# A recurrent attention kernel: the left rows' output projection in matmuls of 512 columns, with six of its passes moved into the next step

## The chip, the cores and the metric

The kernel runs on one core of a Trainium2 chip. The metric is the device time of one execution in microseconds; for the kernel before it is 2106.89 us, the median of three runs (2102.43 to 2125.25). The profile is of one execution with a span of 2098.7 us. TensorE is the engine for matmuls, VectorE, ScalarE and GpSimd work elementwise, and SyncE issues the stream of weights.

## The reference: what is computed

Two independent branches are added to the input. Branch A is an attention layer that walks over 2048 rows in 64 segments of 32 rows. Eight memory rows stand before each segment, and the first eight rows of a segment's output are the next segment's memory. So the segments can only be done one after the other, and each needs all four weight matrices (8 MB each in bf16).

```python
for s in range(n_seg):                                # 64 segments
    xs = x[:, s * seg_len:(s + 1) * seg_len, :]       # 32 rows of 1024
    h = jnp.concatenate([mem, xs], axis=1)            # 8 + 32 rows
    q, k, v = (jnp.einsum('btd,dhe->bhte', h, W) for W in (Wq, Wk, Wv))   # 32 heads of 128
    scores = jnp.einsum('bhqe,bhke->bhqk', q, k) * scale   # then mask and softmax -> p
    o = jnp.einsum('bhqk,bhke->bhqe', p, v)
    o = jnp.einsum('bhte,hed->btd', o, Wo)            # output projection, 4096 -> 1024
    mem = o[:, :M, :]                                 # the next segment's memory
    outs.append(o[:, M:, :])
```

Branch B sends the two rows with the highest router score through a gated feed-forward block, and runs at the kernel's end.

## The kernel before

A step s works on 32 rows that TensorE takes as one block: 8 memory rows and 24 of the segment's rows. The last eight rows of each segment, the **left rows**, are not on the recurrence's path for q, k and v, so they are gathered from four segments (a group G; j = s mod 4) into another block of 32 rows. The left rows' q is computed in the step with j = 2, their k in j = 3, both for the group ahead, and their v in j = 0. Their output projection, `project_left`, is done in the step with j = 3, when the attention of all four segments is there (OTL), into the PSUM tile WL.

The weights are cut into 64 granules of 512 KB (48 for q, k and v in six phases of eight, 16 for Wo). 42 stay in SBUF, 22 are streamed anew in every step, through six slots (tile g). Three of the streamed ones bring only half: the other half is held in PSUM and copied by ScalarE. A slot is loaded again when `used` is called after the last matmul that reads it.

```python
N_RES = 42
N_SLOT = 6
PHASES = [(0, 0), (1, 0), (0, 1), (1, 1), (2, 0), (2, 1)]     # (matrix, half): q, k, q, k, v, v

# one step: the six phases, each of eight granules
for p, (mat, half) in enumerate(PHASES):
    ...
    for kc in range(KC):
        g = 8 * p + kc
        Gv = granule(g)
        for jq in range(4):      # four column groups of the array, 512 columns each
            nc.tensor.matmul(PSm[32 * jq:32 * jq + 32, :], lhsT=ST[:, kc, :], rhs=Gv[:, 512 * jq:512 * (jq + 1)], ...)
        ...                      # a left pass with the same granule, where this step has one
        for fn in hooks.pop((p, kc), []):
            fn()                 # other work, hung in at a place (phase, granule)
    if mat < 2:
        XB = two.tile([P, 512], BF16, tag="xb", name="XB")
        nc.scalar.copy(out=XB[:, :], in_=PSm[:, :])
        hooks.setdefault((p + 1, (3, 2, 3, 2)[p]), []).insert(0, lambda ...: transposes(m, h, b))
```

The output projection comes after the phases. Its matmuls have 256 columns, because four column groups share the 1024 outputs:

```python
def project(PS, w, Gv, lhs, last=False, first=False):
    for hs in range(2):                   # two heads in a granule
        h = 2 * w + hs
        for g in range(4):                # four column groups
            nc.tensor.matmul(PS[32 * g:32 * g + 32, 0:256], lhsT=lhs(h),
                             rhs=Gv[:, D * hs + 256 * g:D * hs + 256 * (g + 1)], ...)

def project_left(w, Gv, WL=WL if j == 3 else None):
    nonlocal n_wl
    project(WL, w, Gv, lhs_left, first=(n_wl == 0))
    n_wl += 1

for w in range(16):
    if w == 4:
        attend(1, 0)                      # value products of the second half of the heads
    if w == 8:
        attend(1, 1)
    Gv = granule(48 + w)
    project(WO, w, Gv, lhs_main, w == 15)
    if j == 3:
        ...
        if 48 + w in streamed:            # w = 0, 2, 5, 8, 11, 14
            project_left(w, Gv)
        else:
            behind.append((w, Gv))        # ten resident ones
        if w in (10, 12, 14):
            project_left(*behind.pop(0))
    used(48 + w)

OB = one.tile([P, 512], BF16, tag="vm", name="OB")
nc.scalar.copy(out=OB[:, 0:P], in_=WO[:, 0:P])
nc.vector.tensor_copy(out=OB[:, P:256], in_=WO[:, P:256])
```

When a step's projection is done, OB must be copied and the memory rows transposed into the next step's operand (`mem_to_st`) before the next step begins. Passes that don't depend on it (`fill`) are put on either side of the transposes: in the steps with j = 3 the seven left passes that remain, with j = 1 and 2 passes of the next step's left q or k.

```python
if j == 3:
    fill = [lambda w=w, Gv=Gv: project_left(w, Gv) for w, Gv in behind]
elif j == 1 or j == 2:
    ...                                   # left q or k passes of the next step
for fn in fill[:len(fill) // 2]:
    fn()
if s + 1 < NSEG:
    mem_to_st(OB, nxt["st"])
for fn in fill[len(fill) // 2:]:
    fn()
if j == 3:
    ...
    def left_store(G=G, WL=WL, X=XLT):
        residual(WL, X[:, 0:256], P, False)          # adds x + xn by four matmuls of 256 columns
        OL = one.tile([P, 512], BF16, tag="vm", name="OL")
        nc.scalar.copy(out=OL[:, 0:256], in_=WL[:, 0:256])
        ...                                          # four stores
    todo += [((0, 6), left_norm), ((1, 6), left_store)]   # places in the next step
```

Of the kernel before, what the change touches and what calls it, by code (L numbers as in the profile page):

```python
# [8 lines left out]
BF16 = mybir.dt.bfloat16  # L9
F32 = mybir.dt.float32  # L10
U32 = mybir.dt.uint32
ALU = mybir.AluOpType
# [15 lines left out]
def kernel(  # L28
# [16 lines left out]
    nc = tc.nc  # L45
    P = 128
    Bsz, S, D = A_x.shape
    H, E = A_Wq.shape[1], A_Wq.shape[2]
    M = A_mem0.shape[1]
    SEG = int(A_seg_len)  # L50
# [8 lines left out]
    XM = SEG - M  # L59
# [32 lines left out]
    two = ctx.enter_context(tc.tile_pool(name="two", bufs=2, reuse_waits="tile"))  # L92
# [8 lines left out]
    IDENT = const.tile([P, P], BF16, name="IDENT")  # L101
# [3 lines left out]
    for q0 in range(0, P, 32):  # L105
        nc.vector.tensor_copy(out=SPREAD[q0:q0 + 32, :, :],
                              in_=IDENT[q0:q0 + 32, q0:q0 + 32].unsqueeze(2).to_broadcast([32, 32, 4]))
# [140 lines left out]
    def load_left(G, queue=nc.gpsimd, again=False):  # L248
        X = two.tile([P, 512], BF16, tag="xb", name="XL") if again else one.tile([P, 512], BF16, tag="vm", name="XL")
        for sl in range(4):  # L250
            r0 = (4 * G + sl) * SEG + XM
            queue.dma_start(out=X[32 * sl:32 * sl + 32, 0:256],
                                in_=x2[r0:r0 + XL, :].rearrange("r (g c) -> (r g) c", g=4))
        return X
# [19 lines left out]
    def norm_left(G, X):  # L274
        PS = psT.tile([P, 2], F32, tag="t", name="PS")
        for b in range(0, P, 32):
            nc.tensor.matmul(PS[b:b + 32, :], lhsT=SPREAD[b:b + 32, 4 * XM:P], rhs=MS[b:b + 32, G, :],
                             start=True, stop=True, tile_position=(b, b), skip_group_check=True)
        norm(X[:, 0:256], X[:, 256:512], PS, P)
# [19 lines left out]
    def residual(PS, Z, n, start):  # L299

        for g in range(4):
            nc.tensor.matmul(PS[32 * g:32 * g + 32, 0:256], lhsT=IDENT[0:n, g::4], rhs=Z, start=start, stop=not start,
                             tile_position=(0, 32 * g), skip_group_check=True)
# [26 lines left out]
    def granule(g):  # L330
        return take("w", g) if g in streamed else res_tiles[g]

    def used(g):
        if g in streamed:
            fetch()
# [9 lines left out]
    todo = []  # L345
# [55 lines left out]
    def left_pass(L, kc, Gv):  # L401

        for jq in range(4):
            nc.tensor.matmul(L["ps"][32 * jq:32 * jq + 32, :], lhsT=cur["stl"][:, kc, :],  # L404
                             rhs=Gv[:, 512 * jq:512 * (jq + 1)], start=(not L["had"]), stop=(len(L["had"]) == KC - 1),
                             tile_position=(0, 32 * jq))
        L["had"].append(kc)

    def left_bank():
        return {"ps": psL.tile([P, 512], F32, tag="accl", name="PSl"), "had": []}  # L410

    begun = {}
    for s in range(NSEG):
        G, j = divmod(s, 4)
# [114 lines left out]
        def attend(half, ph):  # L529
            if half not in OT:  # L530
                OT[half] = one.tile([P, 4, 4, SEG], BF16, tag=("qt", "kt")[half], name="OT")
            PTm, PTl = PTs[half]

            if ph == 0:
                OA[half] = psA.tile([P, 512], F32, tag="acc", name="OA")
            OB1 = psT.tile([P, 4 * NK], F32, tag="t", name="OP")
            c1 = 256 if half == 0 else 256 * ph
            OP = (OA[half][:, c1:c1 + 4 * NK], OB1[:, :])
            for il in range(4):
                for jl in range(2):  # L540
                    q0 = 32 * (2 * ph + jl)
                    c0 = half * 512 + il * P
                    o = OP[jl][:, il * NK:(il + 1) * NK]
                    nc.tensor.matmul(o, lhsT=VM[half][q0:q0 + 32, il * P:(il + 1) * P], rhs=PTm[q0:q0 + 32, il, 0:NK],  # L544
                                     start=True, stop=False, tile_position=(q0, 0), skip_group_check=True)
                    nc.tensor.matmul(o, lhsT=VL[q0:q0 + 32, c0:c0 + P], rhs=PTl[q0:q0 + 32, il, 0:NK],  # L546
                                     start=False, stop=True, tile_position=(q0, 0), skip_group_check=True)
            h0 = 16 * half + 8 * ph
            for jl in range(2):
                ov = OP[jl].rearrange("p (i q) -> p i q", i=4)  # L550
                copy = nc.vector.tensor_copy if half == 1 and jl == 1 else nc.scalar.copy
                copy(out=OT[half][:, 2 * ph + jl, :, :], in_=ov[:, :, 0:SEG])  # L552
                copy(out=OTL[:, h0 + 4 * jl:h0 + 4 * jl + 4, j, :], in_=ov[:, :, SEG:NK])
# [41 lines left out]
        for p, (mat, half) in enumerate(PHASES):  # L595
# [3 lines left out]
            lag, behind = 2 if j == 0 else 0, []  # L599
# [3 lines that stand above are left out]
                for jq in range(4):  # L603
                    nc.tensor.matmul(PSm[32 * jq:32 * jq + 32, :], lhsT=ST[:, kc, :], rhs=Gv[:, 512 * jq:512 * (jq + 1)],  # L604
                                     start=(kc == 0), stop=(kc == KC - 1), tile_position=(0, 32 * jq))
# [40 lines left out]
        if j == 3:  # L646
            WL = psL.tile([P, 512], F32, tag="accl", name="WL")

        def project(PS, w, Gv, lhs, last=False, first=False):
            for hs in range(2):  # L650
                h = 2 * w + hs
                for g in range(4):
                    nc.tensor.matmul(PS[32 * g:32 * g + 32, 0:256], lhsT=lhs(h),  # L653
                                     rhs=Gv[:, D * hs + 256 * g:D * hs + 256 * (g + 1)], start=(first and hs == 0),
                                     stop=(last and hs == 1), tile_position=(0, 32 * g), skip_group_check=True)
# [7 lines left out]

        n_wl, behind = 0, []

        def project_left(w, Gv, WL=WL if j == 3 else None):
            nonlocal n_wl
            project(WL, w, Gv, lhs_left, first=(n_wl == 0))
            n_wl += 1

        for w in range(16):
            if w == 4:
                attend(1, 0)
# [5 lines that stand above are left out]
                if w == 2:  # L679
                    XLT = load_left(G, again=True)  # L680
                if 48 + w in streamed:
                    project_left(w, Gv)
                else:
                    behind.append((w, Gv))
                if w in (10, 12, 14):
                    project_left(*behind.pop(0))
            used(48 + w)

        OB = one.tile([P, 512], BF16, tag="vm", name="OB")
# [8 lines left out]
        todo = [((0, 2), store)]  # L698

        fill = []  # L700
        nl = left_of(s + 1) if s + 1 < NSEG else {}
        if j == 3:
            fill = [lambda w=w, Gv=Gv: project_left(w, Gv) for w, Gv in behind]
        elif j == 1 or j == 2:
            for mat in nl:
                begun[mat] = left_bank()
                fill = [lambda kc=kc, g=8 * mat + kc, L=begun[mat]: left_pass(L, kc, res_tiles[g])
                        for kc in range(KC) if 8 * mat + kc not in streamed]
# [6 lines left out]
        if j == 3:  # L715

            def left_norm(G=G, X=XLT):
                norm_left(G, X)

            def left_store(G=G, WL=WL, X=XLT):  # L720
                residual(WL, X[:, 0:256], P, False)
                OL = one.tile([P, 512], BF16, tag="vm", name="OL")
                nc.scalar.copy(out=OL[:, 0:256], in_=WL[:, 0:256])
                o4 = out2[4 * G * SEG:4 * (G + 1) * SEG, :].rearrange("(s r) d -> s r d", s=4)
                for g in range(4):
                    nc.gpsimd.dma_start(out=o4[:, XM:SEG, 256 * g:256 * (g + 1)], in_=OL[32 * g:32 * (g + 1), 0:256])

            todo += [((0, 6), left_norm), ((1, 6), left_store)]
        if s + 1 < NSEG:
# [12 lines left out]
    for w in range(2):  # L742
# [3 lines left out]
        for kc in range(KC):  # L746
            for fh in range(2):
                Gt = take("gu", w, kc, fh)

                for q in range(4):  # L750
                    nb = 4 if q < 2 else 3
                    nc.tensor.matmul(GU[w, fh][32 * q:32 * q + 32, 0:nb * P], lhsT=XSP[:, kc, :],
                                     rhs=Gt.rearrange("p (b q c) -> p q b c", q=4, c=P)[:, q, 0:nb, :],
                                     start=(kc == 0), stop=(kc == KC - 1), tile_position=(0, 32 * q))
# [10 lines left out]
    for fh in range(2):  # L765
        for p1, c0, c1 in ((P, 0, 3 * P), (64, 3 * P, 4 * P)):
            nc.scalar.activation(out=SG[0:p1, fh, c0:c1], in_=GU[0, fh][0:p1, c0:c1], func=ACTF.Silu)
            nc.vector.tensor_tensor(out=HB[0:p1, fh, c0:c1], in0=SG[0:p1, fh, c0:c1], in1=GU[1, fh][0:p1, c0:c1],
                                    op=ALU.mult)
# [7 lines left out]
    for i in range(FC // 2):  # L777
        Gt = take("dn", i)
        for a in range(2):
            fh, r = divmod(2 * i + a, FC // 2)  # L780
            b, q = divmod(r, 4)
            for dh in range(2):
                nc.tensor.matmul(YP[dh][0:2, :], lhsT=HT[:, 4 * fh + b, q, :],
                                 rhs=Gt[:, a * D + dh * 512:a * D + (dh + 1) * 512],
                                 start=(i + a == 0), stop=(2 * i + a == FC - 1))
        fetch()
    NEW = fin.tile([2, D], BF16, name="NEW")
    for dh in range(2):
        c = slice(512 * dh, 512 * (dh + 1))
# [40 lines left out]
```

## Time and profile before

| what | value |
|---|---|
| time, median of three | 2106.89 us |
| span of the profiled execution | 2098.7 us |
| TensorE busy: matmuls, weight loads | 1740.0 us, 898.2 us |
| VectorE, ScalarE, GpSimd busy | 747.4, 712.7, 540.9 us |
| DMA over the span | 768.74 MB, mean 366 GB/s |
| chain that ended last: DMA, TensorE | 50%, 39% |
| left projection: 2048 matmuls of 256 columns, busy | 58.4 us (resident granules), 44.0 us (streamed) |
| left q, k and v: 3072 matmuls of 512 columns, busy | 183.1 us, 103.1 us |

In the profile, busy times are shares of one engine's own time, and several engines work at once. PE is TensorE's matmuls, PEld its weight loads, DVE is VectorE, ACT ScalarE, POOL GpSimd, SP SyncE, DVEq and the like an engine's sequencer. Matmuls overlap in the array, so a group's busy time is the union of its matmuls, not their sum. "L653" is a line of the kernel; all matmuls of `project` have this one line, and are told apart by the tile that they write (OA for the main rows, which WO is a name of, and WL for the left ones). A wait's releaser is the thing that came last; "issue" is a wait for nothing that the profile shows. The granted clock is the part of full speed that the array had. A step ends, for this text, where the first copy into OB starts; the 64 of them lie from 114.92 to 2037.51 us, 30.5 us apart on average. The tail after the last is the end of branch B.

### The profile page before, as it was taken

The numbers are of one execution on the slowest core, as the hardware profiler recorded it, in microseconds if no ns is written. First come the engines' busy times: TensorE is split into PE (matmuls) and PEld (weight loads), VectorE is DVE, ScalarE is ACT, GpSimd is POOL, SyncE is SP. The second block draws the span as 40 slices with busy tenths as digits, with TensorE's granted clock in tenths as the row PEclk, the third lists the DMA queues.
The fourth block names the chain that finished last, engine by engine and source line by source line (L and its number), as shares of the span: only waits on it lengthen the run. The fifth ranks groups of instructions, "written<-read, shape, count | busy, mean of one in ns | idle before, by whom it ended". The sixth has DMA issues, their size and how long they took to land.

```text
span 2098.7 us, 82755 instructions
## 1 busy us (share of the span) xinstructions
PE 1740.0 (83%) x36202; PEld 898.2 (43%) x36202; DVE 747.4 (36%) x2328; ACT 712.7 (34%) x1738; POOL 540.9 (26%) x1030
## 2 busy tenths in 40 slices
PE   3578898888889888888888888898898889888775
PEld 1234444444444444444444444444454444444341
DVE  5523332333333233333333333332333333333430
ACT  3633333333333333333333333333333333333320
POOL 4422223222222322222132222223222222222210
PEclk8689999999999999999999999999999999999986
DMA  9999999999999999999999999999999999999998
GB/s 356 334 380 384 360 383 352 389 343 377 373 363 382 350 383 345 364 382 356 367 354 391 360 379 373 373 385 344 385 369 363 373 380 391 321 388 356 362 340 343
DMA packets 294351, 768.74 MB, mean 366 GB/s; under 512 B 37458, under 2 KB 42770, under 8 KB 293988
## 3 DMA queue, kind: packets, MB, share of 16 engines
q1 hardware_dynamic: 267652, 732.79, 93.5%
q0 software_dynamic: 23520, 26.06, 3.7%
q8 instruction: 283, 4.64, 0.8%
q10 hardware_dynamic: 2816, 4.59, 0.6%
q14 instruction: 80, 0.66, 0.1%
HBM read 750.68 MB, written 12.59 MB: 364 GB/s over the span
## 4 chain that ended last, share of the span: by engine, by line
DMA 50%; PE 39%; DVE 4%; issue 4%; ACT 2%; POOL 1%; ACTq 0%; DVEq 0%; SPq 0%; POOLq 0%
DMA g<-in_A_Wo_dram 19%; PE PSm L604 18%; DMA g<-in_A_Wv_dram 12%; DMA g<-in_A_Wq_dram 11%; PE PSl L404 6%; PE OA L653 5%; PE WL L653 3%; PE PTq L444 2%; DMA g<-in_A_Wk_dram 2%; DMA XL<-in_A_x_dram 1%; DMA out_dram<-OB 1%; DMA wres<-in_A_Wo_dram 1%; DMA g<-in_B_w_up_dram 1%; PE SPS L488 1%; PE OA L544 1%
## 5 line engine op out<-in xcount | busy, mean ns | idle before, releaser
L604 PE MATMUL PSm<-wres,ST 128*32 128x512 bf16 x8192 | 746.7, 394 | 6.8 <-DVE ST L309 5.1
L604 PE MATMUL PSm<-g,ST 128*32 128x512 bf16 x4096 | 417.1, 394 | 92.1 <-DMA g<-in_A_Wv_dram 42.9
L604 PEld LDWEIGHTS <-ST 128*32 128x32 bf16 x12288 | 294.8, 97 | 422.6 <-issue 192.3
L653 PEld LDWEIGHTS <-OT 128*32 128x32 bf16 x8192 | 221.6, 99 | 167.1 <-issue 151.7
L220 ACT COPY g<-HELD 128x1024 bf16<-128x1024 bf16 x189 | 191.3, 1012 | 213.0 <-PE PSm L604 146.8
L653 PE MATMUL OA<-wres,OT 128*32 128x256 bf16 x5120 | 244.3, 284 | 21.8 <-issue 16.0
L623 ACT CAST XB<-PSm 128x512 bf16<-128x512 f32 x256 | 150.2, 587 | 280.2 <-PE PSm L604 275.5
L653 PE MATMUL OA<-g,OT 128*32 128x256 bf16 x3072 | 162.9, 283 | 94.0 <-DMA g<-in_A_Wo_dram 82.0
L404 PE MATMUL PSl<-wres,STL 128*32 128x512 bf16 x2048 | 183.1, 391 | 13.8 <-DVE XBl L627 13.2
L340 POOL DMA_DIRECT2D QKL<-qkl_d x126 | 92.1, 731 | 256.6 <-issue 113.9
L552 ACT CAST OT<-OA 128x128 bf16<-128x128 f32 x256 | 68.2, 266 | 262.5 <-PE OP L546 259.7
L476 POOL COPY KT<-QKL 128x128 bf16<-128x128 bf16 x128 | 37.8, 295 | 427.6 <-PE OA L653 316.4
L695 POOL DMA_DIRECT2D out_dram<-OB x256 | 129.9, 514 | 52.1 <-DVE OB L691 35.7
L552 DVE CAST OT<-OP 128x128 bf16<-128x128 f32 x128 | 37.3, 292 | 260.0 <-PE OP L546 260.0
L493 DVE TENSOR_REDUCE NM<-SPS 128x8 f32<-128x320 f32 x128 | 62.9, 491 | 179.1 <-PE SPS L488 179.1
L404 PEld LDWEIGHTS <-STL 128*32 128x32 bf16 x3072 | 84.2, 98 | 88.6 <-issue 37.4
L635 ACT CAST VM<-PSm 128x512 bf16<-128x512 f32 x128 | 77.2, 603 | 121.2 <-PE PSm L604 121.2
L451 DVE COPY KT<-PTq 128x512 bf16<-128x512 bf16 x128 | 54.0, 422 | 168.9 <-PE PTq L444 168.8
L404 PE MATMUL PSl<-g,STL 128*32 128x512 bf16 x1024 | 103.1, 391 | 9.3 <-DVE XBl L627 6.7
L444 PE MATMUL PTq<-IDENT,XB 128*128 128x128 bf16 x1024 | 103.2, 224 | 8.4 <-ACT XB L623 3.9
L691 DVE CAST OB<-OA 128x128 bf16<-128x128 f32 x64 | 18.7, 292 | 252.8 <-ACT OB L690 198.2
L444 PEld LDWEIGHTS <-XB 128*128 128x128 bf16 x1024 | 59.9, 98 | 111.1 <-ACT XB L623 53.3
(140 smaller groups left out, 2338.9 us busy)
## 6 DMA issues: line engine op xcount, KB each, us to landing
g<-in_A_Wo_dram SPq DMA_DIRECT2D x384, 512.0 KB, 7.0
g<-in_A_Wq_dram SPq DMA_DIRECT2D x321, 512.0 KB, 7.5
g<-in_A_Wk_dram SPq DMA_DIRECT2D x257, 512.0 KB, 6.4
g<-in_A_Wv_dram SPq DMA_DIRECT2D x257, 512.0 KB, 6.9
g<-in_A_Wq_dram SPq DMA_DIRECT2D x63, 256.0 KB, 6.1
g<-in_A_Wk_dram SPq DMA_DIRECT2D x63, 256.0 KB, 5.7
g<-in_A_Wv_dram SPq DMA_DIRECT2D x63, 256.0 KB, 7.1
qkl_d<-QS POOLq DMA_DIRECT2D x64, 128.0 KB, 5.8
```

Source lines behind the costliest of these rows:

```text
L220: nc.scalar.copy(out=t[:, 1024:2048], in_=held[what[1]][:, :].bitcast(BF16))
L340: nc.gpsimd.dma_start(out=t[:, :, :], in_=qkl_d[s // 4][:, half, :, s % 4, :].rearrange("m p c -> p m c"))
L404: nc.tensor.matmul(L["ps"][32 * jq:32 * jq + 32, :], lhsT=cur["stl"][:, kc, :], rhs=Gv[:, 512 * jq:512 * (jq + 1)], start=(not L["had"]), ...
L444: nc.tensor.transpose(out=PTq[:, il, :, :].rearrange("p j r -> p (j r)"), in_=XB[:, il * P:(il + 1) * P], identity=IDENT[:, :])
L451: nc.vector.tensor_copy(out=keys(half)[:, :, 0:32], in_=pv)
L493: nc.vector.tensor_reduce(out=NM[:, :], in_=S8, axis=AX.X, op=ALU.max, negate=True)
L552: copy(out=OT[half][:, 2 * ph + jl, :, :], in_=ov[:, :, 0:SEG])
L604: nc.tensor.matmul(PSm[32 * jq:32 * jq + 32, :], lhsT=ST[:, kc, :], rhs=Gv[:, 512 * jq:512 * (jq + 1)], start=(kc == 0), stop=(kc == KC - ...
L623: nc.scalar.copy(out=XB[:, :], in_=PSm[:, :])
L635: nc.scalar.copy(out=VM[half][:, :], in_=PSm[:, :])
L653: nc.tensor.matmul(PS[32 * g:32 * g + 32, 0:256], lhsT=lhs(h), rhs=Gv[:, D * hs + 256 * g:D * hs + 256 * (g + 1)], start=(first and hs == ...
L695: nc.gpsimd.dma_start(out=out2[s * SEG:s * SEG + XM, 256 * g:256 * (g + 1)], in_=OB[32 * g:32 * g + XM, 0:256])
```

## The change

The left rows' projection no longer splits the 1024 output columns over four column groups. It splits them over two, in matmuls of 512 columns, and gives the other two column groups to the second head of the granule. So even heads add up in WL's partitions 0 to 63, odd heads in 64 to 127. Four matmuls do what eight did. The two halves must be added at the end: ScalarE copies the lower half to SBUF in float32 and VectorE adds it to the upper one, in two pieces. The residual goes into partitions 0 to 63, and two stores of 512 columns take the place of four of 256.

The second part moves work. The three passes at w = 10, 12 and 14 are gone from the projection's loop. Of the ten passes with resident granules, four are left around the memory rows' transposes, and six are hung into the next step, four in its first q phase and two in its first k phase, where that step streams weights. The aim is fewer instructions for TensorE, and less work in the step that has most of it.

```diff
-        def project_left(w, Gv, WL=WL if j == 3 else None):
+        def project_left(w, Gv, WL=WL if j == 3 else None, lhs=lhs_left):
+
             nonlocal n_wl
-            project(WL, w, Gv, lhs_left, first=(n_wl == 0))
+            for hs in range(2):
+                for a in range(2):
+                    q0 = 64 * hs + 32 * a
+                    nc.tensor.matmul(WL[q0:q0 + 32, :], lhsT=lhs(2 * w + hs),
+                                     rhs=Gv[:, D * hs + 512 * a:D * hs + 512 * (a + 1)], start=(n_wl == 0), stop=False,
+                                     tile_position=(0, q0), skip_group_check=True)
             n_wl += 1
@@ in the projection's loop
-                if w in (10, 12, 14):
-                    project_left(*behind.pop(0))
@@ after OB
         if j == 3:
-            fill = [lambda w=w, Gv=Gv: project_left(w, Gv) for w, Gv in behind]
+            fill = [lambda w=w, Gv=Gv: project_left(w, Gv) for w, Gv in behind[:4]]
+            spots = [(0, 1), (0, 3), (0, 5), (0, 7), (1, 1), (1, 4)]
+            todo += [(pk, lambda w=w, Gv=Gv, go=project_left: go(w, Gv)) for pk, (w, Gv) in zip(spots, behind[4:])]
+            assert len(behind) == 10
@@ in left_store
-                residual(WL, X[:, 0:256], P, False)
+                for g in range(4):
+                    a, c = 32 * (g // 2), 256 * (g % 2)
+                    nc.tensor.matmul(WL[a:a + 32, c:c + 256], lhsT=IDENT[:, g::4], rhs=X[:, 0:256], start=False,
+                                     stop=True, tile_position=(0, a), skip_group_check=True)
+                T = two.tile([P, 512], BF16, tag="xb", name="T").bitcast(F32)
                 OL = one.tile([P, 512], BF16, tag="vm", name="OL")
-                nc.scalar.copy(out=OL[:, 0:256], in_=WL[:, 0:256])
+                for c in range(2):
+                    cs, ps = slice(256 * c, 256 * (c + 1)), slice(64 * c, 64 * (c + 1))
+                    nc.scalar.copy(out=T[ps, :], in_=WL[64:P, cs])
+                    nc.vector.tensor_tensor(out=OL[0:64, cs], in0=WL[0:64, cs], in1=T[ps, :], op=ALU.add)
                 o4 = out2[4 * G * SEG:4 * (G + 1) * SEG, :].rearrange("(s r) d -> s r d", s=4)
-                for g in range(4):
-                    nc.gpsimd.dma_start(out=o4[:, XM:SEG, 256 * g:256 * (g + 1)], in_=OL[32 * g:32 * (g + 1), 0:256])
+                for a in range(2):
+                    nc.gpsimd.dma_start(out=o4[:, XM:SEG, 512 * a:512 * (a + 1)], in_=OL[32 * a:32 * (a + 1), :])
```

## The prediction

> **What bounds the kernel now.** I read the page's DMA lines first, then the same stretch for each of the four kinds of step, then TensorE's waits, then the timeline at the longest wait. Call a step by s mod 4: kind 3 is the step in which the left rows are projected, kind 0 the one after it. The page says that the weights' stream never rests for long:
>
> ```profile
> q1 hardware_dynamic: 267652, 732.79, 93.5%
> q8 instruction: 283, 4.64, 0.8%
> HBM read 750.68 MB, written 12.59 MB: 364 GB/s over the span
> ```
>
> All queues together fill 98.6% of the 16 engines' span (93.5, 3.7, 0.8, 0.6 and 0.1%). A step must bring 22 streamed granules, 19 of 512 KB and 3 of 256 KB. But the rate isn't the same in all steps. Stretches from one OB copy to the next, kinds 1, 2, 3, 0 in this order (columns: stretch, length, busy time and count of each engine, granted clock, DMA share, GB/s):
>
> ```profile
> 1093.01:1122.50 29.49, 23.60 (x489) 11.83 (x489) 10.95 (x36) 9.50 (x24) 8.06 (x16) 1.00 1.03 398
> 1122.50:1152.03 29.53, 25.73 (x555) 13.18 (x551) 10.44 (x32) 10.78 (x27) 6.52 (x13) 1.00 1.01 377
> 1152.03:1184.26 32.23, 28.87 (x627) 15.87 (x623) 11.02 (x33) 10.67 (x26) 8.47 (x17) 0.95 1.03 396
> 1184.26:1214.92 30.66, 26.42 (x603) 14.04 (x595) 10.68 (x35) 10.76 (x27) 8.41 (x16) 1.00 0.91 311
> ```
>
> The reader is to see that kinds 1 and 2 take 29.5 us at a full DMA, that kind 3 is nearly 3 us longer with TensorE busiest, and that kind 0 is long although both TensorE and the DMA have room. Over all such stretches the means are 29.85, 29.93, 31.35 and 30.97 us, 122.1 us for a group of four. In kind 0 the DMA slows: from 2 to 12 us after the OB copy of a kind 3 step the mean over 15 groups is 259 GB/s at a share of 0.79. In the same place after kinds 1 and 2 it is 366 and 378 GB/s. Why, the waits tell (engine, line, waited for: total us, times, longest):
>
> ```profile
> PE OA L653 <- DMA g<-in_A_Wo_dram: 82.0, 138, 2.5
> PE OA L653 <- issue: 25.5, 25, 2.6
> PE WL L653 <- issue: 22.2, 15, 2.5
> ```
>
> The first line is TensorE waiting for Wo's granules, in kinds 1 and 2 above all (1.84 and 2.21 us a step, 0.41 in kind 3). The other two are waits for nothing that the profile shows, on the projection's line. Split by kind they are 2.03 us a step in kind 3, 0.85 in kind 0 (in the passes after OB), and below 0.1 in kinds 1 and 2. One of them, in the timeline:
>
> ```profile
> 1174.45 0.29 PE L653 MATMUL OA<-wres,OT 128*32 128x256 bf16 x4 [0.34 <-issue]
> ...
> 1177.95 0.29 PE L653 MATMUL WL<-g,OTL 128*32 128x256 bf16 x4
> 1180.76 0.40 PE L653 MATMUL WL<-g,OTL 128*32 128x256 bf16 x4 [2.52 <-issue]
> 1180.95 0.64 PE L653 MATMUL OA<-wres,OT 128*32 128x256 bf16 x8
> 1181.38 0.64 PE L653 MATMUL WL<-wres,OTL 128*32 128x256 bf16 x8
> ```
>
> Two such waits end 6.3 us apart (1174.45 and 1180.76); in other groups too (319.20 and 325.39; 805.36 and 811.67; 930.88 and 937.09). After the long one a pass takes 0.43 us instead of 0.22. What the DMA does around it:
>
> ```profile
> 1178.20:1180.70 2.50, 0.04 (x4) 0.00 (x0) 0.00 (x0) 0.00 (x0) 0.42 (x1) 1.00 1.03 399
> 1180.70:1184.80 4.10, 4.04 (x84) 2.91 (x84) 0.24 (x1) 0.27 (x1) 0.29 (x1) 0.58 1.02 360
> 1186.00:1196.00 10.00, 9.52 (x180) 4.26 (x172) 3.89 (x14) 5.49 (x8) 5.99 (x12) 1.00 0.81 250
> ```
>
> While TensorE stands still the stream runs on at 399 GB/s and fills its six slots; then it can only follow TensorE's releases, and runs at 250 GB/s for ten microseconds. My reading: TensorE loses time in kind 3 for want of instructions, and the DMA loses the same time a little later for want of slots.
>
> [...] 72,406 instructions of TensorE are 283 blocks, the 283 packets of q8. [...] the waits 6.3 us apart fit one block per 6.3 us beside a full weight stream. [...]
>
> **The change part by part** (per group of four; 16 groups).
>
> 1. Array time of the 16 left passes. In the timeline a pass of eight 256-column matmuls starts 0.22 us after the one before (1172.39, 1172.61, 1172.83); a q pass of four 512-column ones 0.215 us (1186.17, 1186.38). All four column groups stay in use. Saved: 16 x 0.005 = 0.1 us. The wider matmul itself brings nothing.
>
> 2. Instructions. Each matmul has its weight load, so a pass falls from 16 to 8: 128 a group, 2,048 of 72,406 in all. What counts is the dense stretch, from the first value product to the end of the passes after OB. Before: 128 (value products) + 32 (the last four v passes) + 8 (residual) + 256 (main projection) + 9 x 16 + 7 x 16 (left) + 4 = 684, or 2.7 blocks. After: 128 + 32 + 8 + 256 + 6 x 8 + 4 x 8 + 4 = 508, 2.0 blocks. A kind 1 step has some 468 there (its five passes after OB are q passes of 8) and shows 0.22 us of such waits. So of 2.03 + 0.85 = 2.9 us I leave 0.3: saved 2.6 us.
>
> 3. Clock. From 10 us before to 2 us after OB the granted clock averages 0.95, in the next 10 us 0.957: some 0.6 + 0.4 = 1.0 us lost. Dips after waits for Wo remain (0.98 and 0.94 in kinds 1 and 2). Saved, estimated: 0.6 us.
>
> 4. Six passes move. Three leave kind 3's loop and three the place after OB: 6 x 0.215 = 1.3 us earlier into the next q phase; then the six cost 1.3 us among q and k. Net zero for TensorE, but they land where it would soon wait for weights.
>
> 5. Added. The residual has two column groups at a time instead of four: 0.1 us. The end of WL was one ScalarE copy of 0.37 us, and k's copy stood right behind it:
>
> ```profile
> 1191.00 0.37 ACT L723 CAST OL<-WL 128x256 bf16<-128x256 f32 x1 [0.61 <-PE WL L302]
> 1191.27 0.59 ACT L623 CAST XB<-PSm 128x512 bf16<-128x512 f32 x1
> ```
>
> Its transposes started at 1191.91, 0.05 us after that copy ended at 1191.86. A second copy puts them 0.3 us later. The two adds on VectorE fall into its idle 1.81 us before the K copy. Only two passes on either side of the memory rows' transposes, not three and four: 0.1 us. Stores: two of 32 KB for four of 16 KB, on GpSimd, off the path. Sum: 0.5 us.
>
> TensorE's side: -0.1 - 2.6 - 0.6 + 0.5 = -2.8 us a group. The DMA's side: the slow ten microseconds could run at the 372 GB/s of the other kinds, 10 x (1 - 259/372) = 3.0 us. The two are one loss seen from either end and don't add; the smaller counts, with something off for waits for weights that come back in kind 3: 2.6 us a group. There are 15 whole groups and half a gain at the last, whose end flows into the streamed expert weights: 15.5 x 2.6 = 40 us. 2106.9 - 40 = about 2066.
>
> **The rivals.** (a) The stream bounds everything: freed TensorE time only turns into waits for granules. For it: the share of 98.6%, and 82 us of waits for Wo. Against it: 259 GB/s in kind 0. Then 0 to 10 us, about 2100. (b) The fetch still bounds: 472 instructions stand in kind 3's stretch up to OB (1.8 blocks, 11.6 us at 6.3). That stretch took 13.9 us before (1170.4 to 1184.3); less 2.0, 0.6 and three passes it would take 10.6. For it: q and k passes use a block in 6.9 us, so little is in stock when the stretch begins. Against it: kind 1 passes the same count nearly without it. Then half the gain, about 2086. (c) The new work in q and k hurts: six passes, the second copy and the late transposes fall into a stretch that TensorE bounds now (9.52 of 10 us busy). Then kind 0 keeps its 31 us, and only kind 3 gains: about 2080. (d) Better: clock dips vanish and the DMA gets all of its 3.3 us and more of kind 0's second half, where it runs at 333 GB/s: about 2045.
>
> **Range and chances.** 2% is 42 us, at 2065: my sum lies on that line. Losses and rivals (a) to (c) weigh a little more than (d), yet the trace shows both losses plainly. **2066 us**, 2042 to 2090 eight times in ten; faster by over 2%: 0.47, within 2%: 0.51, slower: 0.02.
>
> **What would show it.** Step 2: waits for issue on the projection's lines from 47.7 us to under 10. Step 3: clock near 1.00 around kind 3's OB. The sum: kind 3 near 29.6 us, kind 0 near 30.0, kinds 1 and 2 unchanged; 2 to 12 us after OB over 330 GB/s; waits for Wo up in kind 3. Step 5: a wait of k's transposes for XB of some 0.3 us. I am wrong if issue waits stay, or if they go and the sum of the four kinds stays at 122 us.

## The result, and the profile after

The changed kernel takes 2044.91 us (median of four runs, 2041.02 to 2057.13), against 2107.81 us before: a ratio of 0.9693 with a 95% interval of 0.9633 to 0.9754. That is 63 us by the medians. The two profiles differ by 43 us, because the profiled execution of the changed kernel (2057.13 us) was its longest one and that of the kernel before (2100.34 us) one of its shorter ones. A second profile of the changed kernel has a span of 2047.0 us.

The page after, its DMA queues and traffic:

```profile
q1 hardware_dynamic: 267652, 732.79, 94.8%
q8 instruction: 275, 4.51, 0.8%
HBM read 750.68 MB, written 12.59 MB: 371 GB/s over the span
```

The same bytes come, only faster: 371 GB/s instead of 364. A block, here and in the prediction, is the 256 instructions of TensorE that there are to each packet of q8: 72,557 recorded ones to 283 packets before (72,404 of them matmuls and weight loads), 70,509 to 275 after. Eight blocks are gone. The stretches of one group of four, kinds 1, 2, 3 and 0, with the columns of before:

```profile
1068.60:1099.09 30.49, 24.28 (x485) 12.54 (x489) 10.95 (x36) 9.50 (x25) 8.06 (x16) 0.96 1.03 394
1099.09:1128.02 28.93, 25.73 (x555) 12.93 (x551) 10.44 (x32) 10.96 (x27) 6.52 (x13) 0.99 0.99 366
1128.02:1157.89 29.87, 27.03 (x579) 13.79 (x571) 11.01 (x33) 10.68 (x26) 8.48 (x17) 1.00 1.03 398
1157.89:1187.97 30.08, 26.80 (x587) 13.70 (x579) 11.52 (x37) 11.12 (x29) 7.33 (x14) 1.00 0.99 349
```

Kind 3 has lost over 2 us, and kind 0 has a full DMA share (0.99 instead of 0.91). Over all steps the kinds now take 30.01, 30.08, 29.33 and 29.98 us in the order 1, 2, 3, 0; a group takes 119.4 us instead of 122.1, and 118.9 us in the second profile. From 2 to 12 us after the OB copy of kind 3 the stream runs at 380 GB/s in the mean over 15 groups (259 before), and the clock in the 22 us around that copy is 1.00 in all of them (in 14 of 15 in the second profile). TensorE's waits after:

```profile
PE OA L653 <- DMA g<-in_A_Wo_dram: 89.3, 160, 2.3
PE PSm L604 <- DMA g<-in_A_Wv_dram: 33.4, 62, 2.0
PE PTq L444 <- ACT XB L623: 22.1, 29, 2.7
PE OA L653 <- issue: 13.2, 19, 1.2
PE PSm L604 <- DMA g<-in_A_Wk_dram: 7.8, 14, 1.4
PE WL L672 <- issue: 3.5, 5, 1.3
```

The waits for issue on the projection's lines are down from 47.7 to 16.7 us, and the longest from 2.6 to 1.3 us. The waits for Wv and Wk are down too (42.9 and 20.5 before). A new wait has come: k's transposes for XB, 22.1 us where the kernel before had 3.9. The timeline of ScalarE and VectorE at the end of WL shows its cause:

```profile
1165.38 0.37 ACT L736 COPY T<-WL 64x256 f32<-64x256 f32 x1 [0.78 <-PE PSm L604]
1166.23 0.37 ACT L736 COPY T<-WL 64x256 f32<-64x256 f32 x1 [0.48 <-DVE OL L737]
1166.62 0.59 ACT L623 CAST XB<-PSm 128x512 bf16<-128x512 f32 x1
...
1165.78 0.42 DVE L737 TENSOR_TENSOR OL<-WL,T 64x256 bf16<-64x256 f32 x1 [1.24 <-ACT T L736]
1166.63 0.42 DVE L737 TENSOR_TENSOR OL<-WL,T 64x256 bf16<-64x256 f32 x1 [0.43 <-ACT T L736]
```

ScalarE's second copy waits for VectorE's first add, though the two touch other partitions of T and other columns of WL. So the end of WL is a chain of copy, add, copy, and k's XB stands behind it. Why the second copy waits for the add was not tested.

That the stream runs out of slots can be read from the queue's own waits. These are SyncE's waits before it could load a slot, for the left passes that read it, before and after:

```profile
SPq L222 <- PE WL L653: 97.8, 90, 3.9
SPq L222 <- PE WL L672: 55.5, 74, 1.4
```

SyncE waited 42 us less for the left passes, and at most 1.4 us at a time instead of 3.9.

### The profile page after: what moved, and what is told of

It is laid out like the page before. It is cut to its first block, busy times and chain, and to the rows that moved or that the text cites. A ratio compares the mean times of both kernels' runs of the same rounds, so it can differ in the third digit from the quotient of the medians.

```text
span 2055.5 us, 80692 instructions
## 1 busy us (share of the span) xinstructions
PE 1723.8 (84%) x35178; PEld 862.0 (42%) x35178; DVE 759.6 (37%) x2360; ACT 718.1 (35%) x1754; POOL 523.2 (25%) x998
## 3 DMA queue, kind: packets, MB, share of 16 engines
q1 hardware_dynamic: 267652, 732.79, 94.8%
## 4 chain that ended last, share of the span: by engine, by line
DMA 54%; PE 36%; DVE 3%; issue 3%; ACT 2%; POOL 1%; ACTq 0%; DVEq 0%; POOLq 0%; SPq 0%
DMA g<-in_A_Wo_dram 21%; PE PSm L604 19%; DMA g<-in_A_Wq_dram 12%; DMA g<-in_A_Wv_dram 10%; PE PSl L404 5%; PE OA L653 3%; DMA g<-in_A_Wk_dram 3%; PE PTq L444 2%; DMA out_dram<-OB 2%; DMA XL<-in_A_x_dram 1%; PE WL L672 1%; DMA QKL<-qkl_d 1%; DMA wres<-in_A_Wo_dram 1%; PE SPS L488 1%; DMA g<-in_B_w_up_dram 1%
## 5 line engine op out<-in xcount | busy, mean ns | idle before, releaser
L604 PE MATMUL PSm<-g,ST 128*32 128x512 bf16 x4096 | 414.8, 392 | 67.4 <-DMA g<-in_A_Wv_dram 33.4
L604 PEld LDWEIGHTS <-ST 128*32 128x32 bf16 x12288 | 300.3, 96 | 403.5 <-issue 170.8
L653 PEld LDWEIGHTS <-OT 128*32 128x32 bf16 x8192 | 216.0, 97 | 175.5 <-issue 154.5
L653 PE MATMUL OA<-wres,OT 128*32 128x256 bf16 x5120 | 234.6, 278 | 15.5 <-issue 9.6
L444 PE MATMUL PTq<-IDENT,XB 128*128 128x128 bf16 x1024 | 103.0, 224 | 22.9 <-ACT XB L623 22.1
L464 POOL DMA_DIRECT2D qkl_d<-QS x64 | 36.6, 573 | 266.0 <-ACT QS L460 261.8
```

Source lines behind the costliest of these rows:

```text
L444: nc.tensor.transpose(out=PTq[:, il, :, :].rearrange("p j r -> p (j r)"), in_=XB[:, il * P:(il + 1) * P], identity=IDENT[:, :])
```

## The experiments

My theory was that instructions arriving too late are the loss, and that the loss of TensorE shows again as a stream that has run out of slots. That the late instructions are late blocks shows in the traces. Number all of TensorE's recorded instructions by their start: in the kernel before, all 40 waits for issue on the projection's lines end at instruction 193 or 194 of a run of 256, that is, always at the same place in a block. The 29 waits of over 0.8 us for Wo's granules end at 29 different places. In the changed kernel all 24 such waits for issue end at 193 or 194 again.

The rival was that the moved passes bring the gain, by taking work out of the fullest step. Each run's ratio is to the kernel before on the same chip.

**Wide passes only** (`e1_wide_only`): the new passes in their old places.

```diff
+                if w in (10, 12, 14):
+                    project_left(*behind.pop(0))
-            fill = [lambda w=w, Gv=Gv: project_left(w, Gv) for w, Gv in behind[:4]]
-            spots = [(0, 1), (0, 3), (0, 5), (0, 7), (1, 1), (1, 4)]
-            todo += [...]
+            fill = [lambda w=w, Gv=Gv: project_left(w, Gv) for w, Gv in behind]
```

> The changed kernel with its 512-column passes, but in the old places: three in the projection's loop, seven around the memory rows' transposes, none in the next step. The dense stretch has 128 + 32 + 8 + 256 + 9 x 8 + 7 x 8 + 4 = 556 instructions instead of 684. Instruction theory (the gain comes from fewer instructions in that stretch): waits for issue on the projection's lines fall from 47.7 us to about 12, and most of the gain is there, about 2060 us. Placement theory (the gain comes from moving TensorE's work out of the step that has most of it): little is gained, about 2095 us.

Measured: 2051.59 us, ratio 0.9714 (0.9647 to 0.978). Waits for issue on the projection's lines are 21.2 us, not 12, but no wait is longer than 1.8 us, and the stream after kind 3 runs at 363 GB/s. Of the 60 us that the whole change brings on this chip, 54 are there without any move. The placement theory is out as the main cause.

**Moved passes only** (`e2_narrow_moved`): the new places and layout, in matmuls of 256 columns.

```diff
-            for hs in range(2):
-                for a in range(2):
-                    ...rhs=Gv[:, D * hs + 512 * a:D * hs + 512 * (a + 1)], start=(n_wl == 0)...
+            for c in range(2):
+                for hs in range(2):
+                    for a in range(2):
+                        ...rhs=Gv[:, r0:r0 + 256], start=(n_wl == 0 and c == 0)...
```

> The changed kernel in all but the width: each pass again in eight matmuls of 256 columns, in the new layout and the new places. The stretch has 128 + 32 + 8 + 256 + 6 x 16 + 4 x 16 + 4 = 588 instructions. Instruction theory: waits for issue of 15 to 20 us, about 2070 us, since moving the passes also takes instructions out of the dense stretch. Placement theory: the same as the changed kernel, about 2045 us, whatever the waits for issue.

Measured: 2084.09 us, ratio 0.9871 (0.9804 to 0.9937); waits for issue 40.4 us, stream after kind 3 at 313 GB/s. By the medians the move alone brings about 21 us, and only 6 on top of the wide passes, which is within the scatter of the two runs (2047 to 2057 and 2043 to 2049 us). The instruction theory had the direction, but expected more: 2070 us and 15 to 20 us of waits. The waits fell by only 7 us here, so how much of the 21 us comes from the thinner stretch, and how much from the placement, stays open.

**The changed kernel again** (`e3_after_again`), unedited.

> The changed kernel once more, unedited, to have it on the same chip as the others and a second profile of it. Expected: 2040 to 2050 us, waits for issue under 20 us, and 20 us of waits of k's transposes for XB.

Measured: 2045.17 us, ratio 0.9687 (0.9621 to 0.9752); waits for issue 19.5 us, waits for XB 22.3 us.

**The end of WL later** (`e4_store_late`):

```diff
-            todo += [((0, 6), left_norm), ((1, 6), left_store)]
+            todo += [((0, 6), left_norm), ((2, 3), left_store)]
```

> The changed kernel with the end of WL (residual, two copies, two adds, stores) hung in at phase 2, granule 3, instead of phase 1, granule 6, so that k's copy out of PSUM no longer stands behind the two copies. If the wait of k's transposes (22.1 us in the profile) is on the path: 10 to 20 us faster than the changed kernel, about 2030 us. If the stream of weights hides it: the same time, 2040 to 2045 us, with more waits for granules in its place.

Measured: 2045.31 us, ratio 0.9682 (0.9614 to 0.975). The waits for XB fall from 22.1 to 5.9 us, and the time stays. The waits of this run for XB and for Wv:

```profile
PE PSm L604 <- DMA g<-in_A_Wv_dram: 47.1, 67, 2.0
PE PTq L444 <- ACT XB L623: 5.9, 17, 0.7
```

Wv's granules took over: 47.1 us instead of 33.4. In kind 0 the wait for XB fell from 1.13 to 0.03 us a step, and the waits for Wv and Wk rose from 0.22 to 1.02. TensorE had waited for XB mostly in time in which it would else have waited for weights.

**The wide passes padded** (`e5_wide_padded`): the run with only the wide passes, with a matmul of 8 columns that adds zero behind each of 512.

```diff
+                    nc.tensor.matmul(WL[q0:q0 + 32, 0:8], lhsT=MASK[:, 40:72], rhs=Gv[:, 0:8], start=False, stop=False,
+                                     tile_position=(0, q0), skip_group_check=True)
```

> As the run with only the wide passes (old places, 2052 us), but behind each 512-column matmul stands one of 8 columns that adds zero to WL: the same array work but for 8 columns in 512, and again 16 instructions a pass, 684 in the dense stretch. Instruction theory: the time goes back to near the kernel before, 2085 to 2105 us, with 35 to 50 us of waits for issue on the projection's lines, and the stream slow again after kind 3. Width theory (the wide matmul itself, its weight loads or its PSUM layout are cheaper): it stays at 2050 to 2060 us.

Measured: 2100.99 us, ratio 0.9976 (0.9953 to 1.0). Its waits for issue on the projection's lines, SyncE's waits for the padded left passes, and the stretch from 2 to 12 us after an OB copy of kind 3:

```profile
PE OA L653 <- issue: 20.1, 18, 2.8
PE WL L675 <- issue: 15.0, 8, 2.3
PE WL L672 <- issue: 6.9, 5, 2.2
...
SPq L222 <- PE WL L675: 97.1, 90, 3.6
...
1181.50:1191.50 10.00, 7.49 (x143) 3.26 (x135) 3.67 (x13) 4.84 (x7) 3.53 (x6) 1.00 0.85 270
```

With the width kept and only the count put back, nearly everything is back: 42 us of waits for issue with waits of up to 2.8 us, SyncE's waits for the left passes at 97.1 us, the stream at 257 GB/s in the mean of 15 groups, and 49 of the 54 us. The padding's own time is small: in the timeline a padded pass starts 0.24 us after the one before, against 0.215, which is 0.4 us a group or some 6 us in all. So the gain of the wide passes comes from the number of instructions in the dense stretch. In order of that number, the five kernels are also in order of time and of the stream's rate, though the steps are not even (32 instructions fewer between 588 and 556 go with 32 us, 96 fewer before that with some 20):

| kernel | instructions in the dense stretch | time, us | GB/s after kind 3 |
|---|---|---|---|
| before | 684 | 2107.7 | 259 |
| padded | 684 | 2101.0 | 257 |
| moved only | 588 | 2084.1 | 313 |
| wide only | 556 | 2051.6 | 363 |
| changed (second run) | 508 | 2045.2 | 377 |

**Half a stream** (`e6_before_half_stream`, `e7_after_half_stream`): most streamed granules bring only their first 1024 columns, which the matmuls then read twice. The projections are therefore not the reference's; TensorE's instructions are as many as before. The stream falls from 732.79 to 414.03 MB.

```diff
+                nc.sync.dma_start(out=t[:, 0:1024], in_=granule_dram(g)[:, 0:1024] if g < 48 else
+                                  Wo2[2 * (g - 48) * P:(2 * (g - 48) + 1) * P, :])
-                    rhs=Gv[:, 512 * jq:512 * (jq + 1)]
+                    rhs=cols(Gv, 512 * jq, 512)          # column modulo 1024 in such a granule
```

> The kernel before with about half of the streamed bytes: a streamed granule brings only its first 1024 columns and the matmuls read them twice, so the projections are not the reference's; all instructions of TensorE are the same. If a block of instructions takes 6.2 us because it queues behind the weights' stream: the blocks come 3.5 to 4.5 us apart, the waits for issue fall below 15 us although the waits for granules are gone too, and the time is TensorE's own, some 1800 us. If a block takes its 6 us in any case: 1,131 instructions a step are 4.4 blocks or 27 us, waits for issue turn up in all steps, over 100 us, and the time is 1850 us or more.

> The changed kernel with the same half stream. If the change brings time only through the instruction blocks behind a full stream: with that wait gone it is worth less than 15 us here (some 2 us less array work, against 16 to 20 us of waits of k's transposes for XB). If the fetch is slow in any case: it keeps 40 us or more over the kernel before with half a stream.

Measured: 1797.63 us for the kernel before with half a stream (ratio 0.8535, 0.8478 to 0.8593) and 1807.85 us for the changed one (ratio 0.8552, 0.8487 to 0.8617). The intervals overlap: here the change is worth nothing that shows. If anything it costs a little. The wait of k's transposes for XB, which the full stream covers, is 24.2 us in the changed kernel with half a stream and 6.5 us in the other; that this is the reason is not shown. The waits for issue of the kernel before, with half a stream:

```profile
PE WL L663 <- issue: 7.5, 8, 1.6
PE OA L663 <- issue: 5.7, 10, 1.1
```

They are 13.2 us instead of 47.7, though TensorE hardly waits for branch A's granules any more (2.6 us in all, 169.8 in the kernel before) and the stretch is denser in time (from 10 us before kind 3's OB to 2 us after it matmuls are busy for 11.3 of 12 us in the mean over 15 groups, 9.1 in the kernel before). In the trace's packets of q8, a quarter of the blocks come within 4.8 us of the one before (6.1 us in the kernel before with its full stream). Around kind 1's OB, from 12 us before to 3 us after, 19 of 25 distances are under 5.9 us with half a stream, and none of 19 in the kernel before with its full one. Around kind 3's OB it is 28 of 30, against 14 of 27. Of these 14 (3.7 to 5.6 us), 11 have a wait of TensorE of over 0.8 us inside them, and in the other three the DMA moved only 305 to 326 GB/s; in the 13 longer ones (5.9 to 6.4 us) it moved 393 to 412. So with the same instructions of TensorE the blocks come sooner beside half a stream. What makes a block late beside the full one was not tested further.

**One copy** (`e8_one_copy`), with one add behind it, in OTL's buffer:

```diff
-                T = two.tile([P, 512], BF16, tag="xb", name="T").bitcast(F32)
+                T = one.tile([P, 1024], BF16, tag="otl", name="T").bitcast(F32)
-                for c in range(2): ...                # copy and add, two pieces
+                nc.scalar.copy(out=T[64:P, :], in_=WL[64:P, :])
+                nc.vector.tensor_tensor(out=OL[0:64, :], in0=WL[0:64, :], in1=T[64:P, :], op=ALU.add)
```

> The changed kernel with one ScalarE copy of 64 x 512 in float32 and one VectorE add instead of two of each in turn; the buffer is that of OTL, which is free by then. k's copy then starts about 0.6 us earlier, and the wait of k's transposes falls from 1.3 to some 0.6 us a group. Since taking that wait away altogether changed nothing: 2040 to 2050 us. If the chain were on the path after all: 2030 to 2038 us.

Measured: 2045.79 us, ratio 0.9707 (0.965 to 0.9764). The waits for XB fall to 9.8 us, and the time stays, as with the later end of WL. No version that I ran beats the changed kernel.

## Why the prediction came out as it did

The time predicted was 2066 us with a range of 2042 to 2090; 2044.9 us lies inside, near the low end. The mechanism held; the sum was too small.

- **Bound.** That TensorE loses time for want of instructions and the DMA loses the same time later for want of slots was right. The padded run shows both come back together. With half a stream the waits for issue shrink to 13.2 us and the change gains nothing, so both need the full stream.
- **Step 1** (no gain from the wide matmul itself): right. The padded run keeps the wide matmul and gains next to nothing.
- **Step 2** (2.6 us a group): the waits for issue on the projection's lines fell in kinds 3 and 0 from 2.9 to 0.9 us, so by 2.0. "I leave 0.3" was too hopeful, and the waits in all came to 16.7 us, not under 10.
- **Step 3** (0.6 us): too small. The clock is 1.00 around kind 3's OB in the first profile, so the full 1.0 us came back. With the long waits gone, the dips there went too.
- **Step 4** (six passes, net zero): not tested by itself. The move alone brings 21 us, but it also takes 96 instructions out of the dense stretch, which belongs to step 2; on top of the wide passes it brings 6 us, within the scatter.
- **Step 5** (0.5 us): wrong in size and in weight. I took the second copy to follow the first; it waits for an add, and the wait of k's transposes was 1.1 us a step in kind 0 (1.2 in the second profile), not 0.3. Yet beside the full stream it costs nothing that shows: two runs took most of it away and gained nothing.
- **The sum.** Here a term was mis-sized. I set TensorE's side to -2.8 us and the DMA's to -3.0, let "the smaller" count, and took something off, 2.6 in all. But TensorE's extra waits fall into slack: its waits for Wv and Wk in kind 0 went from 1.80 to 0.22 us a step as the wait for XB came. Counted by what was measured (the 0.1 is the estimate of step 1), TensorE's side is only -0.1 - 2.0 - 1.0 + 1.1 = -2.0 us, and the groups still became 2.7 and 3.2 us shorter in the two profiles. The DMA's side fits that better: 10 x (1 - 259/380) = 3.2 us. Had it stood alone, it would have made 15.5 x 3.2 = 50 us. This is a reading after the fact; no run changed the stream's slow ten microseconds alone. The remaining 13 us of the medians' 63 are not accounted for; the profiles show 43 and 52 us, and only one profile of the kernel before is at hand.
- **Rivals.** (a) was wrong for the whole and right for step 5. (b) was wrong: the fetch no longer bounds the stretch, though 0.9 us of its waits remain; that little would be in stock was my estimate, from 6.9 us in which q and k passes use a block and 6.3 us between two waits. (c) was wrong: kind 0 went to 29.98 us, with the new work in it. (d) named the measured time, but by luck: its clock and its 3.3 us came, the gain in kind 0's second half did not (from 12 us after OB the stream ran at 355 GB/s before and 356 after, in the mean over 15 groups; the 333 that I gave is near that of the one group shown). Waits for Wo in kind 3 rose as expected, from 0.41 to 0.80 us a step. The kinds came out at 29.33 (predicted 29.6) and 29.98 (30.0).

## What to carry to other kernels

A wait for nothing that the profile shows, in a stretch of many small matmuls, can be the instruction fetch, as it was here: count the instructions between two such waits, see whether they end a multiple of one block apart (256 here), and look at the distance of the instruction queue's packets (5.9 to 6.4 us here). Where that is the cause, the same work in fewer and wider instructions can help although the array's time hardly changes (54 us here, with passes 0.21 to 0.22 us apart before and after); moving work to a thinner stretch helped less (21 us). When a stream with few slots is the bound, try to price a change also by the time in which the stream runs slow: here that gave 3.2 us a group and the engine's own waits 2.0, where 2.7 and 3.2 were measured.

## What the runs showed of the hardware

- Beside the full stream (371 GB/s over the span), blocks of 256 instructions around kind 3's OB came 5.9 to 6.4 us apart (20 of 22 distances in the changed kernel), and TensorE waited where it would have used them sooner (up to 1.3 us at a time there, up to 2.6 us in the kernel before). In the kernel before, each of the 22 waits for issue of over 0.8 us on the projection's lines ended 2.2 to 2.7 us after the start of a block's packet, which itself took 0.9 to 1.2 us.
- The blocks' packets came late rather than far ahead. In the kernel before, between the first OB copy and the last, the packet with number k (from 0) started when TensorE had begun between 256 k + 180 and 256 k + 449 instructions, and the 22 long waits all ended at 256 k + 449 or 450. If packet k brings the block that these waits were for, as their ends suggest, none began more than some 270 instructions (450 - 180) before TensorE needed its block; this is an estimate from the count.
- The array's clock fell after some long waits and not after others. Of the 11 waits for issue of over 2 us on the projection's lines in the kernel before, seven (2.13 to 2.61 us) were followed within 1.4 us by 3.4 us at a clock of 0.5, as the one that ended at 1180.76; four (2.06 to 2.46 us) were not. In the first profile of the changed kernel, whose waits for issue reach 1.3 us, it stays at 1.00 around kind 3's OB.
- A ScalarE copy of 64 x 256 from PSUM in float32 took 0.37 us, as long as one of 128 x 256 to bf16; one of 64 x 512 took 0.58 us, less than two of the halves.
